# Fewer and larger transpose DMAs between windowed attention and a gated feed-forward layer

## The chip, the cores and the metric

The kernel runs on one core of a Trainium2 chip. The metric is device time in microseconds, the median of several executions of the same program. The engines are TensorE (PE, with its weight loads shown apart as PEld), VectorE (DVE), ScalarE (ACT), GpSimd (POOL) and SyncE (SP), which here only issues DMAs.

## What is computed

Windowed attention with four sink keys, and then a feed-forward layer with a gate. Sizes: batch 4, 8 heads, 768 positions, head size 64, window 128; 3072 tokens, model width 512, inner width 2048.

```python
scores = (q @ k.transpose(0, 1, 3, 2)) / sqrt(64)
rel = pos[:, None] - pos[None, :]
keep = (pos[None, :] < 4) | ((rel >= 0) & (rel < 128))
a = softmax(where(keep, scores, -1e9))
x = (a @ v).transpose(0, 2, 1, 3).reshape(3072, 512)
h = x @ w_in
out = (h * sigmoid(beta * h)) @ w_out
```

Inputs and output are float32. The products run in bfloat16 with float32 sums.

## The kernel before

The work is cut into 8 half batches of 384 tokens (`hb`, three blocks of 128), and each half batch into 4 units, a unit being two heads. Unit `u` is half batch `u // 4`, pair of heads `u % 4`.

For each half batch: q, k and v are loaded in float32 (`load`, line 543), three DMAs each, and cast to bfloat16 on whichever engine is free (`cast`, line 584). q and k must have the head dimension on partitions, so they are transposed into `qkT`. For half batches 0 to 2 (`CUT = 3`) TensorE does that (`T`, line 651). From the fourth on, SyncE issues crossbar transpose DMAs (`XP`, line 634): one for each of q and k and each block of 128 tokens, so six for a half batch, each with four 128x128 blocks, one block for each unit. Score products (`SC`, line 735) read `qkT` and write PSUM, ScalarE takes the exponential (line 747), GpSimd or VectorE masks (lines 755, 761, 765). The four sink keys have small products of their own (`first_keys`, line 623 on GpSimd, and `SS`, line 777). `AV` (lines 807 and 818) multiplies with v and divides into `onorm` (line 824), tokens on partitions. The feed-forward layer needs it transposed, as `xT`: by TensorE for the first three half batches (`OT`, line 844), then by one transpose DMA for each unit (line 838), of three blocks each. `HQ` is the first product of the feed-forward layer (line 862), with tanh on ScalarE (line 867) and the gate on VectorE (line 869); `OQ` is the second (line 882), whose result is copied and sent out (line 892, from GpSimd, and from SyncE for the last half batch).

The order of all this is not written out by hand. `_program` appends operations as its own clock says that they can run, choosing among transposes, scores, AV, H and O pieces (`head` and `background`); then `Graph.arrange` orders the operations of every engine once more with a list of costs: each has `ns`, and a DMA also `hold`, the time that it keeps its issuing engine. A DMA's landing is put at `dma_free + 1000`, with `dma_free = max(dma_free, at + 1100) + 1.15 * ns`. A q or k transpose has ns 950 and hold 1310, an xT transpose 750 and 1310. `Graph.resolve` turns the dependencies into semaphore waits, and every engine runs its own list in order. An instruction that waits holds back all that stand behind it on that engine.

Gates around the changed DMAs: `qkT` has room for three half batches (NT = 12 units), and `XP` of half batch hb is planned only when its chunk is cast and the units of hb - 2 are all scored; `x16` has two buffers, `onorm` five (NON), `xT` five half batches (NXT).

Of the kernel before, what the change touches and what calls it, by code (L numbers as in the profile page):

```python
# [4 lines left out]
BF16 = mybir.dt.bfloat16  # L5
F32 = mybir.dt.float32
# [356 lines left out]
def _program(nc, G, sb, ps, q, k, v, w_in, w_out, beta, out):  # L363
    NU = 2 * NPAIR
    NSTG, NX, NV, NT, NE, NON, NG, NTT, NOS, NWS = 2, 2, 3, 12, 7, 5, 3, 3, 4, 6
    NXT = 5
# [6 lines left out]
    maskT = sb("maskT", (128, 2, 128), BF16)  # L373
    beta_st = sb("beta_st", (16, 128), F32)
    ident32 = sb("ident32", (16, 16), F32)
    hbeta = sb("hbeta", (128, NM), F32)
    warm = sb("warm", (1, 1), F32)
    headm = sb("headm", (128, 2), BF16)
    xT = sb("xT", (128, 4, NXT * HALF), BF16)
    w_in16 = sb("w_in16", (128, 4, DF), BF16)  # L380
# [6 lines left out]
    vaug = sb("vaug", (128, NK, H, D + 1), BF16, NV)  # L387
    qkT = sb("qkT", (128, NT, 2, HALF), BF16)
    E = sb("E", (128, 4, 2, 128), BF16, NE)
# [5 lines left out]
    own = sb("own", (128, H), F32)  # L395
    onorm = sb("onorm", (128, NK, 2, D), BF16, NON)
    rden = sb("rden", (128, 2 * NK), F32, NON)
# [5 lines left out]
    tt = sb("t", (128, HALF), F32, NTT)  # L403
    osb = sb("osb", (128, NOUT), F32, NOS)
    P = ps("P", (128, 8, 512))

    def add(eng, fn, ns, r=(), w=(), x=(), dma=None, after=(), hold=550, chain=None):
# [111 lines left out]
    def beta_in():  # L519
        G.begin()  # L520
        b_ = take(1)
        add("pe", lambda e: nc.tensor.transpose(P[:, b_[0], 0:NM], beta_st[:, :], ident32[:, :]), 30,
            r=["beta_st", "ident32"], x=[("B", b_[0])])
        add("dve", lambda e: e.tensor_scalar(hbeta[:, :], P[:, b_[0], 0:NM], 0.5, None, ALU.mult), 80,
            w=["hbeta"], x=[("B", b_[0])])
        give(b_)
# [75 lines left out]
    def first_values_pe():  # L602
# [9 lines left out]
        give(bk)  # L612

    def qk_keys(u, name="qkT", every=NT):
        return [(name, u % every, a, c) for a in range(2) for c in range(NK)]

    def first_keys(hb, units):

        ks = hb // 2 % 2
        j0, n = units[0], len(units)  # L620
        z0 = (4 * hb + j0) % NT
        kd = kS[ks][:, 32 * j0:32 * (j0 + n)].rearrange("p (j a w) -> p j a w", a=2, w=16)[:, :, :, 0:NSINK]
        add("gp", lambda e: e.tensor_tensor(
            kd, qkT[:, z0:z0 + n, 1:2, 0:NSINK].to_broadcast([128, n, 2, NSINK]),
            headm[:, :].unsqueeze(1).unsqueeze(3).to_broadcast([128, n, 2, NSINK]), ALU.mult), 200,
            r=[("kS", ks), "headm0", "headm"] + [("qkT", z0 + j, 1, 0) for j in range(n)],
            w=[("kSd", ks, j) for j in units])

    def XP(hb, n, c):

        z0, i = 4 * hb % NT, "qk".index(n)
        src = x16[n][hb % NX][:, c, :, :].rearrange("p h d -> p (h d)")
        dst = qkT[:, z0:z0 + 4, i, c * 128:(c + 1) * 128]
        add("sp", lambda e: e.dma_start_transpose(dst, src), 950,
            r=[(n + "16", hb % NX, j, c) for j in range(4)], w=[("qkT", z0 + j, i, c) for j in range(4)],
            dma=f"x{n}{hb % 3}{c}", hold=1310)
        for j in range(4):
            mark(("qkTu", 4 * hb + j, i, c), ("qkT", z0 + j, i, c))
        if hb % 2 == 0 and (n, c) == ("k", 0):
            first_keys(hb, range(4))  # L640

    def T(u):
# [12 lines left out]
        if len(bs) == 2:  # L655
            for i in range(2):
                mp = P[:, bs[i], :].bitcast(BF16)[:, i * HALF:(i + 1) * HALF]
                any_of(copies(qkT[:, u % NT, i, :].rearrange("p (s j) -> p s j", j=NK),
                              mp.rearrange("p (j s) -> p s j", j=NK), {"dve": 470, "act": 380}),
                       w=[("qkT", u % NT, i, c) for c in range(NK)], x=[("B", bs[i])])  # L660
        else:
            mp = P[:, bs[0], :].bitcast(BF16)
            any_of(copies(qkT[:, u % NT, :, :].rearrange("p a (s j) -> p a s j", j=NK),
                          mp[:, 0:2 * HALF].rearrange("p (a j s) -> p a s j", a=2, j=NK), {"dve": 868, "act": 690}),
                   w=qk_keys(u), x=[("B", bs[0])])
# [48 lines left out]
    def SC(n):  # L714
# [4 lines left out]
        for j, t_ in enumerate(tiles):  # L719
# [3 lines left out]
            for (u, kb), cols in jobs.items():  # L723
                half = u // 4 % 2
                cols.sort()
                own_ = u if kb >= NK * half else u - 4
                kt = qkT[:, own_ % NT, 1, :]
                kc = (kb % NK) * 128
                q0, i0, nq = (cols[0][0] - NK * half) * 128, cols[0][1], len(cols)
                st = cols[1][1] - i0 if nq > 1 else 1  # L730
                for hh in range(2):
                    rows = slice(64 * hh, 64 * hh + 64)
                    bank = P[:, bs[2 * j + hh], :].rearrange("p (s w) -> p s w", w=128)
                    dst = bank[:, i0:i0 + st * (nq - 1) + 1:st, :]
                    add("pe", lambda e, dst=dst, kt=kt, kc=kc, rows=rows, q0=q0, nq=nq, u=u: e.matmul(  # L735
                        dst, kt[rows, kc:kc + 128],
                        qkT[rows, u % NT, 0, q0:q0 + 128 * nq].rearrange("p (s w) -> p s w", w=128),
                        start=True, stop=True), mm_ns(128 * nq) / 2 + 12,
                        r=qk_keys(u) + (qk_keys(own_) if own_ != u else []), x=[("B", bs[2 * j + hh])])
# [31 lines left out]
    def SS(hb, bank):  # L771
# [3 lines left out]
        for j in range(4):  # L775
            u = 4 * hb + j
            add("pe", lambda e, j=j, u=u: e.matmul(  # L777
                P[32 * j:32 * j + 32, bank, q0:HALF], kS[ks][:, 32 * j:32 * j + 32], qkT[:, u % NT, 0, q0:HALF],
                start=True, stop=True), 100 if j == 0 else (mm_ns(HALF - q0) if j == 3 else 5),
                r=[("kSd", ks, j)] + qk_keys(u), x=[("B", bank)])  # L780
# [16 lines left out]
    def AV(u):  # L797
# [5 lines left out]
        for m, ps in enumerate(parts(u)):  # L803
# [20 lines left out]
        add("dve", lambda e: e.tensor_tensor(  # L824
            onorm[on][:, :, :, :].rearrange("p m h d -> p (m h) d"), av[:, :, 0:D],
            rden[on][:, :].unsqueeze(2).to_broadcast([128, 2 * NK, D]), ALU.mult), dve_ns(HALF),
# [3 lines left out]
    def OT(u):  # L830
        G.begin()
        b, half, hp = where(u)
        on = u % NON
        t0 = (2 * b + half) % NXT * HALF
        if u >= 4 * CUT:
            dst = xT[:, hp, t0:t0 + HALF].rearrange("p (m t) -> p m t", m=NK)
            src = onorm[on][:, :, :, :].rearrange("p m h d -> p (m h d)")
            add("sp", lambda e: e.dma_start_transpose(dst, src), 750, r=[("on", on)],
                w=[("xT", hp, (2 * b + half) % NXT)], dma=f"xo{on}", hold=1310)
            return  # L840
        bs = take(1)
        mp = P[:, bs[0], :].bitcast(BF16)
        for m in range(NK):
            add("pe", lambda e, m=m: nc.tensor.transpose(  # L844
                mp[:, m * 128:(m + 1) * 128], onorm[on][:, m, :, :].rearrange("p h d -> p (h d)"), ident[:, :]),
                mm_ns(128), r=[("on", on), "ident"], x=[("B", bs[0])])
        any_of(copies(xT[:, hp, t0:t0 + HALF], mp[:, 0:HALF], {"dve": 407, "act": 370}),
               w=[("xT", hp, (2 * b + half) % NXT)], x=[("B", bs[0])])
        give(bs)
# [4 lines left out]
    def HQ(T_, m):  # L854
# [3 lines left out]
        bs = take(1)  # L858
        t0 = T_ % NXT * HALF
        hp = P[:, bs[0], 0:HALF]  # L860
        for c in range(4):
            add("pe", lambda e, c=c: e.matmul(  # L862
                hp, w_in16[:, c, m * 128:(m + 1) * 128], xT[:, c, t0:t0 + HALF],
                start=(c == 0), stop=(c == 3)), mm_ns(HALF),
# [47 lines left out]
    OS += [(T_, t, j) for T_ in range(1, NSB) for t in range(3) for j in range(4)]  # L912
    XPS = [(hb, n, c) for hb in range(CUT, NSB) for n in "qk" for c in range(NK)]
    n_cast, n_w, n_x = [0], [0], [0]
    BACKLOG, AHEAD, MARGIN = 6000, 300, 200

    def head(s):
# [26 lines left out]
        elif s == "AV":  # L944
            if i >= NU or i >= done["OT"] + NON or i >= units_scored() or n_cast[0] < 11 + 9 * (i // 4):
                return None
            t, tb = G.at(av_keys(i)), banks_at(1)
            fn = lambda: (AV(i), mark(("onu", i), ("on", i % NON)))
        elif s == "OT":
# [5 lines left out]
            if i // 4 >= NXT and done["H"] < NM * (i // 4 - NXT + 1):  # L955
                return None
            fn = lambda: (OT(i), mark(("xTu", i % 4, i // 4), ("xT", i % 4, i // 4 % NXT)))
        elif s == "H":
# [22 lines left out]
    def background():  # L981
# [3 lines left out]
        while moved:  # L985
# [29 lines left out]

            if n_x[0] < len(XPS):
                hb, n, c = XPS[n_x[0]]
                if n_cast[0] > CASTS.index(XPS[n_x[0]]) and units_scored() >= 4 * (hb - NT // 4 + 2):
                    XP(hb, n, c)
                    n_x[0] += 1  # L1020
                    moved = True
                    if n_x[0] % 6 == 0:
                        done["T"] += 4
# [43 lines left out]
    def beta_load():  # L1067
        add("sp", lambda e: e.dma_start(beta_st[:, :], beta.rearrange("(m p) -> m p", p=128)), 20, w=["beta_st"],
            dma="dbeta", chain=2)
# [93 lines left out]
```

## Time and profile before

| | us |
|---|---|
| median of 7 runs | 227.83 |
| lowest, highest | 226.26, 229.52 |
| profiled execution, in all | 227.83 |
| profiled execution, span | 226.1 |

| group, line | times | busy us | mean ns |
|---|---|---|---|
| first feed-forward product, L862 | 512 | 97.1 | 326 |
| second, L882 | 384 | 96.2 | 379 |
| attention times v, L818 | 352 | 17.8 | 193 |
| scores, L735 | 288 | 14.4 (on top of weight loads 9.4) | 230 |
| gate on VectorE, L869 | 128 | 70.3 | 552 |
| tanh on ScalarE, L867 | 128 | 74.1 | 583 |
| transposes of q and k by DMA, L634 | 30 | | 1269 a median issue |
| transposes of onorm by DMA, L838 | 20 | | 1256 a median issue |

The span is the time from the first to the last instruction of the program in the profiled execution; the device time is 1.7 us longer. TensorE's durations overlap, since a product starts before the end of the one ahead, so the starts tell more than the durations. The chain that ended last is TensorE work for 81% of the span; L882 is 37% of it and L862 33%.

### The profile page before, as it was taken

To read this page: it belongs to the slowest core of one execution; us is meant where nothing else is said; L and a number is where in the kernel's file an instruction comes from. 1 tells how busy PE (TensorE), PEld (TensorE's weight loads), DVE (VectorE), ACT (ScalarE), POOL (GpSimd) and SP (SyncE) were. 2 spreads that over 40 slices of the span, in tenths; PEclk is the share of its full clock that TensorE was granted. 3 is DMA by queue.
4 is the path that set the end of the run, shared out by engine and by line. 5 is a ranking of instruction groups with operands and counts; after the bars stand their busy time and mean duration, and the time that the engine had idled before them with its cause. 6 is when DMAs were issued, how large, how long until landed. Compare 5 with 4: busy or idle time off the path is not lost.

```text
span 226.1 us, 4583 instructions
## 1 busy us (share of the span) xinstructions
PE 215.7 (95%) x1802; PEld 124.0 (55%) x1802; DVE 138.2 (61%) x289; ACT 148.4 (66%) x241; POOL 78.2 (35%) x137
## 2 busy tenths in 40 slices
PE   8796986999999999999999999999999999999994
PEld 6574644656556565646555655545654665555541
DVE  1667879966668575669676644748864564633310
ACT  2595996657984687495577875587666936744431
POOL 6156649024470465048004451037002840000000
PEclk9999999999999999999999999999999999999999
DMA  5999999999989967589949986799448033011112
GB/s 144 240 290 355 323 306 394 392 265 226 159 187 261 193 122 197 128 186 219 197 84 200 213 177 146 148 226 246 106 93 180 0 85 80 0 46 49 46 48 93
DMA packets 96077, 39.86 MB, mean 176 GB/s; under 512 B 82024, under 2 KB 92280, under 8 KB 96056
## 3 DMA queue, kind: packets, MB, share of 16 engines
q1 hardware_dynamic: 94376, 34.07, 65.7%
q0 software_dynamic: 1680, 5.51, 7.5%
q8 instruction: 14, 0.23, 0.4%
q14 instruction: 7, 0.06, 0.1%
HBM read 27.37 MB, written 6.29 MB: 149 GB/s over the span
## 4 chain that ended last, share of the span: by engine, by line
PE 81%; SPq 10%; DMA 3%; DVE 3%; issue 0%; ACT 0%
PE P L882 37%; PE P L862 33%; SPq L543 6%; PE P L735 4%; SPq L554 4%; PE P L818 4%; DMA v_stage<-in_v_dram 3%; DVE E L765 2%; PE P L807 1%; PE P L777 1%; PE P L651 1%; PE P L844 1%; DVE vaug L478 0%; ACT osb L473 0%; DVE onorm L824 0%
## 5 line engine op out<-in xcount | busy, mean ns | idle before, releaser
L867 ACT ACTIVATE t<-P,hbeta 128x384 f32<-128x384 f32 x128 | 74.1, 583 | 48.9 <-PE P L862 44.9
L869 DVE SCALAR_TENSOR_TENSOR g<-t,P 128x384 bf16<-128x384 f32 x128 | 70.3, 552 | 51.6 <-ACT t L867 47.6
L862 PE MATMUL P<-xT,w_in 128*128 128x384 bf16 x512 | 97.1, 326 | 0.7 <-DVE g L869 0.5
L882 PE MATMUL P<-w_out,g 128*128 128x512 bf16 x384 | 96.2, 379 | 0.0
L862 PEld LDWEIGHTS P<-xT,w_in 128*128 128x128 bf16 x512 | 48.4, 98 | 38.9 <-DVE g L869 1.3
L761 POOL TENSOR_SCALAR_AFFINE_SELECT E<-E 128x512 bf16<-128x512 bf16 x60 | 40.2, 691 | 60.0 <-ACT E L747 59.7
L882 PEld LDWEIGHTS P<-w_out,g 128*128 128x128 bf16 x384 | 36.0, 98 | 35.1 <-DVE g L869 0.8
L747 ACT ACTIVATE E<-P 128x1024 bf16<-128x1024 f32 x44 | 43.2, 1026 | 4.1 <-PE P L735 3.7
L892 POOL DMA_DIRECT2D out_dram<-osb x21 | 11.8, 562 | 43.5 <-ACT osb L473 43.3
L818 PE MATMUL P<-vaug,E 128*128 128x65 bf16 x352 | 17.8, 193 | 2.1 <-DVE E L765 1.5
L824 DVE TENSOR_TENSOR onorm<-P,rden 128x384 bf16<-128x384 f32 x32 | 17.8, 558 | 1.1
L473 ACT ACTIVATE osb<-P 128x512 f32<-128x512 f32 x17 | 10.1, 597 | 12.7 <-PE P L882 12.6
L818 PEld LDWEIGHTS P<-vaug,E 128*128 128x128 bf16 x352 | 15.7, 97 | 4.6 <-DVE E L765 2.4
L735 PE MATMUL P<-qkT 64*128 64x128 bf16 (+1 forms) x288 | 14.4, 230 | 0.8 <-DVE qkT L478 0.8
L735 PEld LDWEIGHTS P<-qkT 64*128 64x128 bf16 x288 | 9.4, 94 | 9.5 <-issue 3.9
L807 PE MATMUL P<-vS,ES 128*128 128x130 bf16 x64 | 12.9, 220 | 0.0
L755 DVE TENSOR_TENSOR E<-E,maskS 128x512 bf16<-128x512 bf16 x16 | 7.7, 480 | 8.1 <-ACT E L747 8.1
L478 DVE CAST q<-q_stage 128x512 bf16<-128x512 f32 (+1 forms) x15 | 7.6, 518 | 6.8 <-DMA q_stage<-in_q_dram 6.8
L1073 PE MATMUL P<-ones 128*128 128x256 bf16 x60 | 9.9, 321 | 1.1 <-POOL ones L484 1.1
L478 DVE CAST vaug<-v_stage 128x512 bf16<-128x512 f32 x16 | 7.6, 491 | 1.6 <-DMA v_stage<-in_v_dram 1.6
L473 ACT ACTIVATE qkT<-P 128x384 bf16<-128x384 bf16 (+1 forms) x12 | 6.3, 574 | 3.4 <-PE P L651 3.4
L822 DVE RECIPROCAL rden<-P 128x6 f32<-128x6 f32 x32 | 6.1, 189 | 4.0 <-PE P L818 3.9
(58 smaller groups left out, 117.2 us busy)
## 6 DMA issues: line engine op xcount, KB each, us to landing
v_stage<-in_v_dram SPq DMA_DIRECT2D x24, 256.0 KB, 4.5
out_dram<-osb POOLq DMA_DIRECT2D x21, 256.0 KB, 3.1
q_stage<-in_q_dram SPq DMA_DIRECT2D x15, 256.0 KB, 5.1
k_stage<-in_k_dram SPq DMA_DIRECT2D x15, 256.0 KB, 5.0
wst<-in_moe_w_in_dram SPq DMA_DIRECT2D x5, 512.0 KB, 6.1
wst<-in_moe_w_out_dram SPq DMA_DIRECT2D x4, 512.0 KB, 6.9
g<-in_moe_w_out_dram SPq DMA_DIRECT2D x4, 512.0 KB, 7.1
q_stage<-in_q_dram SPq DMA_DIRECT2D x2, 768.0 KB, 8.7
```

The lines of the kernel that those rows point to most:

```text
L473: return lambda e: e.activation(dst, src, AF.Copy, bias=0.0, scale=scale)
L478: return lambda e: e.tensor_copy(dst, src)
L735: add("pe", lambda e, dst=dst, kt=kt, kc=kc, rows=rows, q0=q0, nq=nq, u=u: e.matmul(dst, kt[rows, kc:kc + 128], qkT[rows, u % NT, 0, q0:q0 ...
L747: add("act", lambda e, src=src, dst_=dst_: e.activation(dst_, src, AF.Exp, bias=0.0, scale=SCALE), act_ns(1024), w=[("E", z)] + [("m", z, ...
L761: alts = {"gp": (lambda e, dd=dd, sg=sg: e.affine_select(dd, dd, [[0, 4], [sg, 128]], ALU.is_ge, 0.0, base=min(sg, 0), channel_multiplier= ...
L807: add("pe", lambda e, m=m, c0=c0: e.matmul(A[:, c0:c0 + 2 * (D + 1)], ES[u // 4 % 2][:, m * 128:(m + 1) * 128], vS[b % 2][:, 2 * hp:2 * hp ...
L818: e.matmul(A[:, c0:c0 + D + 1], E[t_ % NE][:, i, hh, :], vaug[vz][:, kb % NK, 2 * hp + hh, :], start=a, stop=o, skip_group_check=True), 31,
L824: add("dve", lambda e: e.tensor_tensor(onorm[on][:, :, :, :].rearrange("p m h d -> p (m h) d"), av[:, :, 0:D], rden[on][:, :].unsqueeze(2) ...
L862: add("pe", lambda e, c=c: e.matmul(hp, w_in16[:, c, m * 128:(m + 1) * 128], xT[:, c, t0:t0 + HALF], start=(c == 0), stop=(c == 3)), mm_ns ...
L867: add("act", lambda e: e.activation(tt[ti][:, :], hp, AF.Tanh, bias=0.0, scale=hbeta[:, m:m + 1]), act_ns(HALF) + 93, r=["hbeta"], w=[("t" ...
L869: add("dve", lambda e: e.scalar_tensor_tensor(gt[T_ % NG][:, m, :], tt[ti][:, :], 1.0, hp, ALU.add, ALU.mult), dve_ns(HALF), r=[("t", ti)] ...
L882: add("pe", lambda e, m=m: e.matmul(P[:, bk, :], gt[T_ % NG][:, m, t * 128:(t + 1) * 128], w_out16[:, m, :], start=(m == 0), stop=(m == NM ...
```

## The change

The six q and k transposes of a half batch become two: one takes all three blocks of q for all four units, one all of k. The `xT` transposes are made for two units at a time. That makes 10 DMAs in place of 30, and 10 in place of 20, with the same bytes.

Three layouts follow. A half batch's slot of `qkT` is flat: for the half batches that TensorE transposes it is ordered unit, q or k, token, as it was; for the others q or k, block, unit, token, so that a unit's three blocks lie 512 elements apart. `xT` is ordered half batch, pair of heads, token. `onorm` comes in pairs of units, with six in place of five. To make room for the sixth, the small staging tile of beta shares the last output buffer `osb`. A slot that still has the old order is given up as a whole: the q transposes of half batches 3 to 5 also wait for the old readers of k.

The planner is given other costs: ns 1300 and hold 1500 for a q or k transpose, 900 and 1300 for a pair of units. `XP` is planned when all three chunks of q, or of k, are cast. `AV` may run ahead by six units, counted from the last full pair that is transposed.

```diff
-    NSTG, NX, NV, NT, NE, NON, NG, NTT, NOS, NWS = 2, 2, 3, 12, 7, 5, 3, 3, 4, 6
+    NSTG, NX, NV, NT, NE, NON, NG, NTT, NOS, NWS = 2, 2, 3, 12, 7, 6, 3, 3, 4, 6
...
-    qkT = sb("qkT", (128, NT, 2, HALF), BF16)
+    qkT = sb("qkT", (128, NT // 4, 8 * HALF), BF16)
...
-    onorm = sb("onorm", (128, NK, 2, D), BF16, NON)
+    onorm2 = sb("onorm", (128, 2, NK, 2, D), BF16, NON // 2)
+    onorm = [onorm2[i // 2][:, i % 2, :, :, :] for i in range(NON)]
...
+    beta_st = osb[NOS - 1][0:16, 0:128]
...
+    XNS, XHOLD, ONS, OHOLD = (1300, 1500, 900, 1300)
...
+    def slot(hb):
+        x = qkT[:, hb % (NT // 4), :]
+        if hb < CUT:
+            return x.rearrange("p (z a c t) -> p a c z t", z=4, a=2, t=128)
+        return x.rearrange("p (a c z t) -> p a c z t", a=2, c=NK, t=128)
+
+    def qk_of(u, i):
+        return slot(u // 4)[:, i, :, u % 4, :]
...
-    def XP(hb, n, c):
+    def XP(hb, n):
 
         z0, i = 4 * hb % NT, "qk".index(n)
-        src = x16[n][hb % NX][:, c, :, :].rearrange("p h d -> p (h d)")
-        dst = qkT[:, z0:z0 + 4, i, c * 128:(c + 1) * 128]
-        add("sp", lambda e: e.dma_start_transpose(dst, src), 950,
-            r=[(n + "16", hb % NX, j, c) for j in range(4)], w=[("qkT", z0 + j, i, c) for j in range(4)],
-            dma=f"x{n}{hb % 3}{c}", hold=1310)
+        src = x16[n][hb % NX][:, :, :, :].rearrange("p c h d -> p (c h d)")
+        dst = qkT[:, hb % (NT // 4), i * 4 * HALF:(i + 1) * 4 * HALF].rearrange("p (b t) -> p b t", t=128)
+        old = [("qkT", z0 + j, 1, c) for j in range(4) for c in range(NK)] if i == 0 and hb < CUT + NT // 4 else ()
+        add("sp", lambda e: e.dma_start_transpose(dst, src), XNS,
+            r=[(n + "16", hb % NX, j, c) for j in range(4) for c in range(NK)],
+            w=[("qkT", z0 + j, i, c) for j in range(4) for c in range(NK)], dma=f"x{n}{hb % 3}", hold=XHOLD, after=old)
...
-                        dst, kt[rows, kc:kc + 128],
-                        qkT[rows, u % NT, 0, q0:q0 + 128 * nq].rearrange("p (s w) -> p s w", w=128),
+                        dst, kt[rows, kc, :], qk_of(u, 0)[rows, q0:q0 + nq, :],
...
         if u >= 4 * CUT:
-            dst = xT[:, hp, t0:t0 + HALF].rearrange("p (m t) -> p m t", m=NK)
-            src = onorm[on][:, :, :, :].rearrange("p m h d -> p (m h d)")
-            add("sp", lambda e: e.dma_start_transpose(dst, src), 750, r=[("on", on)],
-                w=[("xT", hp, (2 * b + half) % NXT)], dma=f"xo{on}", hold=1310)
+            if u % 2:
+                dst = xT[:, x_, hp - 1:hp + 1, :].rearrange("p h (m t) -> p (h m) t", t=128)
+                src = onorm2[on // 2][:, :, :, :, :].rearrange("p u m h d -> p (u m h d)")
+                add("sp", lambda e: e.dma_start_transpose(dst, src), ONS, r=[("on", on - 1), ("on", on)],
+                    w=[("xT", hp - 1, x_), ("xT", hp, x_)], dma=f"xo{on // 2}", hold=OHOLD)
             return
...
-            if i >= NU or i >= done["OT"] + NON or i >= units_scored() or n_cast[0] < 11 + 9 * (i // 4):
+            if i >= NU or i >= (done["OT"] if done["OT"] < 4 * CUT else done["OT"] // 2 * 2) + NON or i >= units_scored() or n_cast[0] < 11 + 9 * (i // 4):
...
-                if n_cast[0] > CASTS.index(XPS[n_x[0]]) and units_scored() >= 4 * (hb - NT // 4 + 2):
-                    XP(hb, n, c)
+                if n_cast[0] > CASTS.index((hb, n, NK - 1)) and units_scored() >= 4 * (hb - NT // 4 + 2):
+                    XP(hb, n)
```

## What was expected of it

> **What bounds the kernel now.** I read the page's engine rows first, then its slices, then the table of windows, then the waits of TensorE from 57 us on, then SyncE's issues. The engine rows say that TensorE's matmul row is busy 95% of the span, but a matmul's modelled end lies beyond the next one's start, so busy alone does not prove a full engine. The windows and the waits do.
>
> ```profile
> span 226.1 us, 4583 instructions
> PE 215.7 (95%) x1802; PEld 124.0 (55%) x1802; DVE 138.2 (61%) x289; ACT 148.4 (66%) x241; POOL 78.2 (35%) x137
> PE   8796986999999999999999999999999999999994
> PEclk9999999999999999999999999999999999999999
> DMA  5999999999989967589949986799448033011112
> ```
>
> ```profile
> 0.00:57.00 57.00, 49.92 (x478) 31.87 (x479) 40.40 (x86) 39.60 (x67) 27.51 (x56) 1.00 1.01 293
> 57.00:218.00 161.00, 161.00 (x1305) 90.15 (x1304) 97.83 (x205) 107.57 (x173) 50.70 (x81) 1.00 0.67 139
> 218.00:226.10 8.10, 4.82 (x23) 1.97 (x21) 0.00 (x0) 1.19 (x2) 0.00 (x0) 1.00 0.25 97
> ```
>
> The columns after the length are busy time of PE, weight load, DVE, ACT and POOL, then the granted clock, the DMA share and GB/s. From 57 to 218 us, where every transpose DMA lies (first 57.5, last 187.2), TensorE has no idle time at all and the clock is 1.00; the answer on TensorE's own waits in that window is an empty list. The starts of the long products agree: four w_out products take 0.86 us from first start to the next group (the groups of the chain), 216 ns each for 512 columns; four w_in products take 0.65, 162 ns for 384 columns, one column in 0.42 ns in both. So the middle is work and not waiting. The TensorE idle time is 7.1 us before 57 us and 3.3 us after the last matmul.
>
> **The DMAs that change.**
>
> ```profile
> L634 SPq DMA_TRANSPOSE qkT<-q x15: 1188/1269/2164, 57.5 to 165.2; - x15
> L634 SPq DMA_TRANSPOSE qkT<-k x15: 1254/1269/2577, 60.7 to 166.5; - x15
> L838 SPq DMA_TRANSPOSE xT<-onorm x20: 1181/1256/1950, 86.8 to 187.2; - x20
> ...
> SPq L838 <- DVE g L869: 23.4, 10, 10.2
> SPq L838 <- DVE onorm L824: 8.5, 3, 3.4
> ```
>
> The three numbers are the shortest, median and longest time in ns that one issue holds SyncE's queue. A qkT transpose moves four 128x128 blocks, an xT one three: 1269 against 1256 ns, so a block more costs 13 ns of issue. The data go fast: in the 0.3 us windows in which only one xT transpose runs (181.0 and 183.0 us) DMA share is 1.06 at 217 to 218 GB/s. A block is 32.8 KB, so 0.15 us a block.
>
> **Part 1: 30 q and k transposes become 10.** Removed: 30 x 1.27 = 38 us of SyncE. Added: 10 issues of twelve blocks, not in this trace. From below an issue costs the fixed 1.27 us; from above it grows with blocks, 3 x 1.27 = 3.8. By the nearest rows it is 1.27 + 8 x 0.013 = 1.37, which I take. [...]
>
> Landing: a four-block transpose lands 2.5 us after its issue when nothing is ahead of it, which is 1.27 of issue, 0.6 of data and 0.6 of the rest. Twelve land at 1.37 + 1.8 + 0.6 = 3.8 us, and with proportional issue at 3.8 + 1.8 + 0.6 = 6.2.
>
> What matters is the last block. Now six issues, which start 1.30 apart at best (four xT ones from 112.75 to 117.95), need 6 x 1.30 + 1.2 = 9.0 us from first issue to last landing; two need 1.37 + 3.8 = 5.2, and 0.4 more because two streams of 1.8 us follow one another. The merged q must wait for its third cast, which is up to 4.8 us later than the first (151.4 and 156.2 us in the last half batch), but the last landing now waits for that cast too. Set that against when it is used. From the last landing to the first score product (line 735) of that half batch there are 7.2, 8.8, 5.7, 8.7 and 4.0 us for half batches 3 to 7; the last is 166.50 + 2.5 = 169.0 to 172.98. So the time removed was covered by 4 us or more of other matmuls, and is worth 0 on the path; if the cover were gone the two holds booked and the measured ones would differ by 2 x (1.37 - 1.5), which is under 0.3.
>
> **Part 2: 20 xT transposes become 10.** SyncE gives up 20 x 1.26 = 25 us and gets 10 x (1.26 + 3 x 0.013) = 13. The bounds for one are 1.26 and 2.5. The first unit of each pair now waits for the second: 0.7 us in the burst at 105.7, 106.4, 107.1, 107.8, at most 2.8 (127.7 to 130.5). The w_in products need all four units, so only the second counts, and it lands 2.4 + 3 x 0.16 = 2.9 us after its issue, 0.5 later than now. Cover: last landing to the first w_in product of that half batch (counted, 64 products each) is 5.4, 2.4, 3.2, 4.1 and 3.3 us. The smallest is 119.1 to 121.5, and there the four transposes stood behind six qkT issues until 112.75 although their data were ready at 108.4; that queue is now shorter by 6 x 1.30 - 2 x 1.37 = 5.1 us. Worth 0 too; if the cover were gone, 0.5 us at each of five places.
>
> **Part 3: waits.** Behind the pair's wait on SyncE stand the v loads and the next half batch's q and k loads. It waits 31.9 us there already (the two rows above), and 38 + 25 - 14 - 13 = 36 us come free in the same queue, so the loads go earlier rather than later. On POOL the sink keys (line 623, twice, 238 ns) wait for all of k in place of its first third: some 4 us later, with mask operations and output DMAs behind it. POOL is 35% busy, and the product that reads the keys comes at 99.9 and 154.0 us, at least 12 us after k has landed. The added wait on old k readers falls on products that ended before 83 us, at least 20 us before the q that needs it: 0. A sixth onorm buffer makes the reuse distance in pairs no shorter than before: 0.
>
> **Part 4: reads with another step.** The 180 score products and 20 sink products of half batches 3 to 7 read qkT in runs of 128 columns, 256 bytes, which are apart by 1 KB now. No row has such a read. A gain is excluded: the columns are as many. From above, if each jump cost 50 ns (no jump is shown; a 128-column pair of products takes 54), 40 products with one jump and 12 with two would cost 3.2 us. The products already write in steps at full pitch, so I take 0.
>
> **Part 5: another order.** Lines of the planner are fed other costs (1300/1500 and 900/1300), so from the first changed issue on (57 us) the order of all engines may differ; before it I expect no change. TensorE's products are the same in number. What order can move is the entry into the half-array score products: the next start after a w_out product is 310 ns off in place of 216 (the idle rows of weight load before line 735, 0.3 to 0.4 us, are its sign). At about 0.19 us for entry and exit, three bursts more or fewer are 0.6 us.
>
> Sum: 0 + 0 + 0 + 0, give or take 0.6. The profiled execution has span 226.1 and 227.83 us in all, which is also the median of the seven runs (226.26 to 229.52). So 227.8. [...]
>
> **Rivals.** *A new wait for the merged transposes (slower).* The planner books 2 x 1.5 us of SyncE where it booked 6 x 1.31, and may bring the scores forward by 4.9 us. If the issue really grows with the blocks (3.8), nothing of that is real, and the streaming adds 1.2: 6.1 late against covers of 4.0 to 8.8, so 2.1 us at half batch 7 and 0.4 at 5; the pairs behind (2.5 held, 1.3 booked) are each 1.2 late, twice, against 2.4 to 5.4, which adds about 1 where the replanned order is tight: 3.5 us, 231.3. It decides from an issue of about 2.9 us. For it: no twelve-block issue is in the trace, and held issues reach 2.6. Against: 13 ns a block. Chance 0.22, with part 4's upper end in it.
>
> *The freed queue helps (faster).* There are 0 us of TensorE waits to take in the window that changes; fewer bursts give 0.6, and the remaining idle lies before 57 us or behind the last product. Over 1% is 2.3 us, which I can find nowhere; chance 0.05, at 225.3.
>
> *The change hardly happens.* The planner may keep the same order of products behind the same gates (scores done, buffers free), with half the DMAs: 227.8, inside the main case. Main case in all 0.73, own range 226.6 to 229.2.
>
> **The numbers.** About 1% is what a measurement of this kernel can tell from no change. Faster by more than that: 0.05 from the faster case and 0.01 of the main one. Slower: 0.22 and 0.01 of the main one, less 0.01 of the slow rival that ends under 1%. Same: 0.72. The range leaves out the faster case and the worse half of the slow one: 226.0 to 231.2.
>
> **What would show it.** Right: no waits in TensorE's list from 57 to 218 us; ten q and k issues of about 1.4 us, landing in about 4; ten pair issues of 1.3 landing in about 3. Wrong: issues near 3 us or more, or a TensorE or weight load wait on a transpose of q, k or onorm; a pitch above 54 ns a pair in the score products of late half batches; idle slices of PE after slice 10; or a busy PE before 57 us that differs from 49.9.

## The result, and the profile after

The changed kernel takes 229.51 us (median of 24 runs, 228.17 to 232.18) against 227.66 before (61 runs); the ratio is 1.0086, with a 95% interval of 1.0067 to 1.0106. It is slower by 1.85 us. The forecast was no change, at 227.8. Some executions take 2 to 3 us longer, most of them at a lower granted clock (four of the kernel before took 230.22 to 230.93 us at 0.982 to 0.985, beside a median of 227.70); the ratios leave them out, and so are not quite the quotients of the medians.

The page of the changed kernel, profiled at 228.57 us in all. Line numbers moved: 634 is 646 now, 838 is 855, 735 is 751, 862 is 878 and 882 is 898.

```profile
span 226.8 us, 4544 instructions
PE 215.7 (95%) x1802; PEld 123.5 (54%) x1802; DVE 139.8 (62%) x290; ACT 147.3 (65%) x240; POOL 77.5 (34%) x137
PE   8887886999999999999999999999999999999994
PEclk9999999999999999999999999999999999999999
DMA  5999999999999999999999999531130211011112
```

TensorE does the same 215.7 us of work. The DMA row is full up to slice 25 and then nearly empty, where before it had holes in the middle and work up to slice 31: the loads do go earlier. The table of windows of the same kernel:

```profile
0.00:57.00 57.00, 49.32 (x477) 31.44 (x478) 41.62 (x85) 39.26 (x67) 27.54 (x56) 1.00 1.04 290
57.00:218.00 161.00, 160.76 (x1302) 89.75 (x1301) 98.17 (x206) 106.56 (x172) 49.97 (x81) 1.00 0.69 140
218.00:226.80 8.80, 5.67 (x27) 2.35 (x24) 0.00 (x0) 1.45 (x3) 0.00 (x0) 0.97 0.23 89
```

In the stretch that the change was meant for, TensorE idles for 161.00 - 160.76 = 0.24 us, of which the view of its waits from 57 us on shows one of 0.2:

```profile
PE P L898 <- DVE g L885: 0.2, 1, 0.2
```

That can't be 1.85. The first 57 us have 0.6 us less TensorE work in them than before (49.92), though there no engine's list of instructions differs from before but in the name of beta's tile: the first row that differs stands at about 57 us. The changed DMAs (issue in ns: shortest, median and longest):

```profile
L646 SPq DMA_TRANSPOSE qkT<-q x5: 1497/1579/2879, 61.4 to 136.5; - x5
L646 SPq DMA_TRANSPOSE qkT<-k x5: 1575/2808/3892, 63.1 to 132.5; - x5
DMA to landing us min/median/max: 3.8/5.2/6.2
...
L855 SPq DMA_TRANSPOSE xT<-onorm x10: 1209/1392/2053, 92.2 to 174.6; - x10
DMA to landing us min/median/max: 2.7/3.9/6.5
```

### The profile page after: what moved, and what is told of

Read it like the earlier page. It is cut to its first block, busy times and chain, and to the rows that moved or that the text cites. A ratio compares the mean times of both kernels' runs of the same rounds, so it can differ in the third digit from the quotient of the medians.

```text
span 226.8 us, 4544 instructions
## 1 busy us (share of the span) xinstructions
PE 215.7 (95%) x1802; PEld 123.5 (54%) x1802; DVE 139.8 (62%) x290; ACT 147.3 (65%) x240; POOL 77.5 (34%) x137
## 4 chain that ended last, share of the span: by engine, by line
PE 76%; SPq 7%; DMA 7%; DVE 5%; ACT 3%; issue 1%; POOL 0%
PE P L898 35%; PE P L878 31%; DMA k_stage<-in_k_dram 7%; SPq L545 5%; PE P L751 4%; PE P L834 3%; ACT E L762 2%; DVE E L780 2%; SPq L556 2%; PE P L823 1%; DVE g L885 1%; DVE onorm L840 1%; PE P L667 1%; DVE qkT L480 1%; PE P L792 1%
## 5 line engine op out<-in xcount | busy, mean ns | idle before, releaser
L885 DVE SCALAR_TENSOR_TENSOR g<-t,P 128x384 bf16<-128x384 f32 x128 | 69.3, 551 | 50.0 <-ACT t L883 47.8
L878 PE MATMUL P<-xT,w_in 128*128 128x384 bf16 x512 | 98.3, 327 | 1.4 <-DVE g L885 1.2
L475 ACT ACTIVATE osb<-P 128x512 f32<-128x512 f32 x19 | 11.3, 597 | 14.1 <-PE P L898 14.1
L480 DVE CAST q<-q_stage 128x512 bf16<-128x512 f32 (+1 forms) x16 | 7.1, 457 | 8.7 <-DMA q_stage<-in_q_dram 8.7
L480 DVE CAST vaug<-v_stage 128x512 bf16<-128x512 f32 x17 | 9.7, 573 | 1.5 <-DMA v_stage<-in_v_dram 1.4
L770 DVE TENSOR_TENSOR E<-E,maskS 128x512 bf16<-128x512 bf16 x16 | 8.5, 539 | 2.9 <-ACT E L762 2.9
L477 POOL TENSOR_SCALAR_AFFINE_SELECT q<-q_stage 128x512 bf16<-128x512 f32 x5 | 3.5, 706 | 17.5 <-DMA q_stage<-in_q_dram 17.5
L780 DVE TENSOR_TENSOR E<-E,maskT 128x512 bf16<-128x512 bf16 x12 | 8.2, 716 | 0.9 <-ACT E L762 0.9
```

Source lines behind the costliest of these rows:

```text
L480: return lambda e: e.tensor_copy(dst, src)
L780: alts["dve"] = (lambda e, dd=dd, tri=tri: e.tensor_tensor(dd, dd, tri, ALU.mult), 335)
L878: add("pe", lambda e, c=c: e.matmul(hp, w_in16[:, c, m * 128:(m + 1) * 128], xT[:, T_ % NXT, c, :], start=(c == 0), stop=(c == 3)), mm_ns( ...
L885: add("dve", lambda e: e.scalar_tensor_tensor(gt[T_ % NG][:, m, :], tt[ti][:, :], 1.0, hp, ALU.add, ALU.mult), dve_ns(HALF), r=[("t", ti)] ...
```

## The experiments

Three theories led the first four runs. A: the planner books the merged transposes too low, so loads are pulled ahead and the casts and masks behind them are late. B: the large streams cost time themselves. C: the coarser release does, since a whole q or k, or a pair of units, must be ready.

**The old bookings on the merged DMAs.**

```diff
-    XNS, XHOLD, ONS, OHOLD = (1300, 1500, 900, 1300)
+    XNS, XHOLD, ONS, OHOLD = (2850, 3930, 1500, 2620)
```

> The changed kernel, but its merged transposes are booked with the planner at what the single ones were booked at in sum: ns 3 x 950 = 2850 and hold 3930 for q or k, 1500 and 2620 for a pair. Theory A (bookings too low: the planner thinks the DMA queue free 4.9 us earlier per half batch, pulls the loads ahead, and puts casts and masks behind loads that land late, so that the gate on VectorE is late): the time returns to that of before, ratio 0.998 to 1.003, the DMA share of 76 to 97 us falls from 1.21 to about 0.75, and the waits of the three casting engines for loads fall from some 28 us in 76 to 148 us to under 5. Rival B (streams of twelve blocks themselves hold up other transfers and land late): the ratio stays at 1.007 to 1.010, whatever is booked. Rival C (waiting for a whole q or a pair, the coarser release): stays at 1.006 or more, with waits that trace to onorm, qkT or xT.

Measured: 228.92 us, ratio 1.0077 (1.0056 to 1.0099). The row of 76 to 97 us, in the changed kernel and then here:

```profile
76.00:97.00 21.00, 20.76 (x190) 12.02 (x188) 15.32 (x36) 16.87 (x27) 10.95 (x19) 1.00 1.21 217
76.00:97.00 21.00, 20.68 (x189) 12.30 (x193) 15.35 (x32) 16.45 (x26) 10.45 (x18) 1.00 0.87 187
```

The DMA share (last but one) fell from 1.21 to 0.87, the time did not come back. Theory A does not carry the loss.

**Low bookings on the single DMAs of before.**

```diff
-        add("sp", lambda e: e.dma_start_transpose(dst, src), 950,
+        add("sp", lambda e: e.dma_start_transpose(dst, src), 433,
...
-            add("sp", lambda e: e.dma_start_transpose(dst, src), 750, r=[("on", on)],
+            add("sp", lambda e: e.dma_start_transpose(dst, src), 450, r=[("on", on)],
```

> The kernel before with its 50 single transposes, but booked in the DMA queue at the merged kernel's sum: ns 433 in place of 950 for q and k, 450 in place of 750 for xT; holds left at 1310. Theory A: slower by 0.4 to 0.9% although no DMA is merged, with a DMA share above 1.0 in 76 to 120 us and waits for loads on the casting engines. Rivals B and C: no change, ratio 0.998 to 1.002.

Measured: 234.98 us, ratio 1.0346 (1.0292 to 1.0399), far more than theory A said. Its waits of TensorE from 57 us on, which the kernel before has none of (the three longest):

```profile
PE P L735 <- DMA qkT<-k: 1.8, 1, 1.8
PE P L807 <- DVE g L869: 1.3, 1, 1.3
PE P L735 <- DVE g L869: 1.3, 1, 1.3
```

The columns are the sum, the number and the longest. A score product waits for a transpose of k, so here a booking that is too low shows in TensorE's list. The changed kernel's list has 0.2 us from 57 us on, and so its bookings are not too low in that sense.

**One half of the change at a time.** First only q and k merged (the xT transposes made one by one again), then only the pairs of xT (six single q and k transposes again).

```diff
-            if u % 2:
-                dst = xT[:, x_, hp - 1:hp + 1, :].rearrange("p h (m t) -> p (h m) t", t=128)
+            dst = xT[:, x_, hp, :].rearrange("p (m t) -> p m t", t=128)
...
```

> Only q and k are merged (2850 booked as 1300, hold 1500); the xT transposes are single as before (750, 1310). Theory A: 3.55 of the 4.9 us less booked per half batch are here (1.15 x (6 x 950 - 2 x 1300)), so about 0.7 of the loss, ratio 1.005 to 1.007. Rival C by pairs: ratio under 1.002, since the pairs are gone. Rival B: 1.006 or more, the large streams being all here.

> Only the xT transposes are made in pairs (900, 1300); q and k have six single DMAs for a half batch as before (950, 1310). Theory A: 1.07 of the 4.9 us less booked (1.15 x (4 x 750 - 2 x 900) is 1.38), so a loss of about a quarter, ratio 1.001 to 1.004. Rival C by pairs: 1.006 or more. Rival B: about 1.001.

Measured: 1.0064 (1.0035 to 1.0093) with q and k alone, 1.0092 (1.0064 to 1.0120) with the pairs alone. Theory A had expected 1.001 to 1.004 of the pairs and theory B 1.001; theory C had expected under 1.002 of q and k alone. Each half by itself costs what the whole does, within the intervals. So the cost was looked for in what the four slow merged kernels (changed, old bookings, and the two halves) share. That is neither DMA, but the storage: each has six onorm buffers and beta in `osb`. Per partition the change takes away 512 bytes (`beta_st`) and adds 768 (onorm) and 32 (a rden of 24 bytes in its slot): `g`, the weight staging `wst`, `t` and `osb`, which are allocated after them, move by 288 = 256 + 32 bytes. By the order of allocation all four began on a multiple of 256 bytes before. No view shows addresses, so what the runs can test is the move; "on the grid" below means the place, up to whole steps of 256 bytes, that these tiles have in the kernel before.

That gave theory L: weight loads that are written 32 bytes off this grid are slower, and they set the pace before 57 us.

**The grid given back to the changed kernel, taken from the kernel before, and given back under the old bookings.**

```diff
-    rden = sb("rden", (128, 2 * NK), F32, NON)
+    rden = sb("rden", (128, 2 * NK), F32, NON - 1)
...
     osb = sb("osb", (128, NOUT), F32, NOS)
+    rden.append(sb("rdenZ", (128, 2 * NK), F32))
```

```diff
     rden = sb("rden", (128, 2 * NK), F32, NON)
+    pad = sb("pad", (128, 8), F32)
```

> The changed kernel with one thing moved: the sixth rden buffer (24 bytes) is allocated last, so that g, the weight staging, t and the output buffers, which the change shifted by 288 bytes a partition, begin on a multiple of 256 bytes again, as before. Every engine's list is the same as in the changed kernel. Theory L (the shift off the 256-byte grid makes the 8.4 MB of weight loads slower, and these set the pace up to 57 us): about 1 us comes back, ratio to before 1.002 to 1.005, last weight landing at 45.4 in place of 45.9 to 47.3 us. Rival A/C (the loss is all in the order after 57 us): no change, ratio 1.007 to 1.010.

> The kernel before with an unused tile of 32 bytes a partition ahead of g, so that g, the weight staging, t and the output buffers begin 32 bytes off the 256-byte grid, as in the changed kernel. Lists unchanged. Theory L: slower by about 1 us, ratio 1.003 to 1.006, with the last weight landing 0.5 to 2 us later than 45.3. Rival A/C: ratio 0.998 to 1.002.

> The first experiment (merged DMAs booked at the old sums) with the sixth rden moved as well, so aligned. Theory L with a rest that comes from the order: ratio 1.000 to 1.004, since the part from 58.3 us on was 164.9 us there against 164.3 before. Rival A/C: as the first experiment, 1.006 to 1.010.

Measured: 1.0024 (0.9986 to 1.0061) for the changed kernel on the grid, 1.0027 (0.9993 to 1.0061) for the kernel before off it, 1.0031 (1.0007 to 1.0056) for the old bookings on it, against 1.0077. All go the way of theory L, and so do the last landings of a weight in the profiles (44.8 us in the first, 45.85 in the second, against 45.3 before, though this measure does not hold up: 46.6 in a later run with the weights on the grid), but the first two intervals reach to 1, and the second ratio is just under what was expected. The first and third lie below 1.0086 and 1.0077 by 0.6 and 0.5%.

**The staging of q, k and v on the grid as well, and another offset.** The q, k and v staging is 64 bytes off the grid in before and after alike. In the kernel before, rden and `own` were moved ahead of `xT`; in the changed one rden was, with `own` put last. That is 192 bytes in either, so that everything that a load writes is on the grid (other tiles move with it, and `qkT`, which the transposes write, goes off). A third run takes a pad of 64 in place of 32 bytes ahead of `g`.

```diff
+    rden = sb("rden", (128, 2 * NK), F32, NON)
+    own = sb("own", (128, H), F32)
     xT = sb("xT", (128, 4, NXT * HALF), BF16)
...
```

> The kernel before with rden and own (192 bytes in all) allocated ahead of xT in place of after onorm: the float32 staging of q, k and v, 64 bytes off the 256-byte grid in before and in the changed kernel alike, now begins on it, and g, the weight staging and the output buffers stay on it. Lists unchanged. Theory L with a grid of 256 bytes: the loads of q, k and v, most of them rows of 256 bytes, go faster, the first 57 us shrink, ratio 0.985 to 0.997. Theory L with a grid of 64 bytes (32 off costs, 64 off does not): ratio 0.998 to 1.002, and the rate of 5 to 46 us stays near 330 GB/s.

> The changed kernel with rden allocated ahead of xT and own last, so that staging of q, k, v, the weights, g and the output buffers all begin on a multiple of 256 bytes. Lists unchanged. Theory L with a grid of 256 bytes: below the aligned variant of the first alignment run (1.0024), 0.988 to 0.999. With a grid of 64 bytes: 1.001 to 1.005, as there.

> The kernel before with an unused tile of 64 bytes a partition ahead of g: g, the weight staging, t and the output buffers 64 bytes off the 256-byte grid. Lists unchanged. Grid of 256 bytes: as with the shift of 32, 1.003 to 1.006 and 308 to 320 GB/s in 5 to 46 us. Grid of 64 bytes: 0.998 to 1.002 and 325 to 337 GB/s.

Measured: 227.07 us and 0.9968 (0.9939 to 0.9998) for the kernel before, 226.93 us and 0.9952 (0.9924 to 0.9980) for the changed one, 1.0040 (1.0018 to 1.0062) for the pad of 64. So 64 bytes off cost as 32 do within the intervals, and a grid of 64 bytes is excluded. No run has an offset of 128, so the runs by themselves do not tell a grid of 256 bytes from one of 128. The mean time of the 78,720 packets of 256 bytes, which are most of these loads and all transposes (counted in the traces), falls from 21.1 ns before to 18.5 in the first of these profiles and 19.0 in the second. The two kernels differ by less than their intervals, and both are slightly faster than the kernel before.

**Which of the moved tiles it is.** Two pads put only `g` and `wst`, or only `t` and `osb`, 32 bytes off; the edit of the first:

```diff
     rden = sb("rden", (128, 2 * NK), F32, NON)
+    pad = sb("pad", (128, 8), F32)
...
+    pad2 = sb("pad2", (128, 56), F32)
     tt = sb("t", (128, HALF), F32, NTT)
```

> The kernel before with 32 unused bytes a partition ahead of g and 224 ahead of t: only g and the weight staging, into which the weight loads are written, lie 32 bytes off the 256-byte grid; t and the output buffers are on it. Lists unchanged. If the weight loads carry the cost: ratio 1.003 to 1.006, as with all of them shifted, and 308 to 320 GB/s in 5 to 46 us. If the output stores or the reads of t carry it: 0.998 to 1.002.

> The kernel before with 32 unused bytes a partition ahead of t: only t and the output buffers lie 32 bytes off the 256-byte grid; g and the weight staging are on it. Lists unchanged. If the weight loads carry the cost: 0.998 to 1.002 and 325 to 337 GB/s in 5 to 46 us. If the output stores or t carry it: 1.003 to 1.006.

Measured: 1.0047 (1.0022 to 1.0072) with only g and the weight staging off, 0.9978 (0.9948 to 1.0007) with only t and the output buffers off. A lower clock is no rival here: among the executions whose granted clock reads 0.996 or more, the mean is 1.1 us above that of the kernel before beside it with all four tiles 32 bytes off, 1.0 with 64, 1.2 with only g and the weight staging off, and 0.3 below it with only t and osb off.

The expected rates of 5 to 46 us do not tell the runs apart: 310 GB/s with the weights off, but also 320 with t and osb off, 321 with all on the grid and 321 with the pad of 64. A shorter stretch does. SyncE issues three weight loads into the spare third of `g`, with q and k of half batch 1 between them, and then v; no issue waits for another engine there. The view of tile `v_stage` from 20 to 23.5 us shows how long a v issue is held behind the weight loads, and how long it then takes to land. The kernel before:

```profile
L543 SPq DMA_DIRECT2D v_stage<-in_v_dram x2: 1145/1726/2307, 21.3 to 22.5; - x2
DMA to landing us min/median/max: 7.1/7.2/7.2
```

The changed kernel:

```profile
L545 SPq DMA_DIRECT2D v_stage<-in_v_dram x2: 1306/1869/2432, 21.1 to 22.5; - x2
DMA to landing us min/median/max: 7.4/7.6/7.7
```

The changed kernel with the sixth rden moved:

```profile
L546 SPq DMA_DIRECT2D v_stage<-in_v_dram x3: 1146/2294/2323, 19.6 to 23.1; - x3
DMA to landing us min/median/max: 6.1/6.9/7.0
```

The kernel before with only g and the weight staging off the grid:

```profile
L545 SPq DMA_DIRECT2D v_stage<-in_v_dram x2: 1314/1870/2426, 21.9 to 23.3; - x2
DMA to landing us min/median/max: 7.4/7.6/7.7
```

And with only t and the output buffers off:

```profile
L544 SPq DMA_DIRECT2D v_stage<-in_v_dram x2: 1146/1714/2281, 21.5 to 22.7; - x2
DMA to landing us min/median/max: 6.8/6.9/6.9
```

The shortest issue in each is the first v load right behind the weights: 1145, 1146 and 1146 ns where the weights lie on the grid, and 1306 and 1314 where they do not. In the other nine profiles the same issue takes 1146 to 1183 on it (four) and 1307 to 1318 off it (five). From the landing of half batch 1's q to that of its first v there are always the same five transfers, 2.5 MB. In the fourteen profiles this takes 7.09 to 7.45 us in the seven with g on the grid, and 7.84 to 8.15 us in the seven with g off it, with no overlap: some 0.7 us more.

The packets say it directly. Their mean times in that stretch, counted in the traces (no view lists them):

| packets | g on the grid, seven profiles | g off it, seven |
|---|---|---|
| weights, 1024 bytes | 46.0 to 46.8 ns | 51.5 to 51.7 ns |
| k, 768 bytes | 36.0 to 39.2 | 41.2 to 41.4 |
| v, 256 bytes | 18.0 to 19.9 | 21.9 to 22.5 |

So the loads beside the weights get slower with them, though their own place is the same; the 36.0 and 18.0 are those of the two runs with their staging on the grid too. What reads the weights does not get slower: the two casts of weights on ScalarE take 1.06 to 1.08 and 1.05 to 1.06 us in all fourteen profiles.

## Why the prediction was wrong

The step that failed is the last sentence of part 3, "A sixth onorm buffer makes the reuse distance in pairs no shorter than before: 0", with part 5's "before it I expect no change" (the order there did stay, the time did not). The buffer was priced as a wait alone. Its bytes, with those of beta's tile, moved the destination of every weight load by 32 bytes off the grid, in the stretch where the DMA share is 1.01 and TensorE idles 7.1 us (both before, up to 57 us). The code gives all sizes, so this could have been counted before. The cost: 1.0086 against 1.0024 on the grid is 0.62%, 1.4 us of the 1.85, give or take 0.4% by the two intervals; the kernel before with only g and the weight staging off pays 0.47% (0.22 to 0.72), 1.1 us.

The traces show the cost in the packets of the weight loads in the stretch above, 51.5 to 51.7 in place of 46.0 to 46.8 ns for 1024 bytes; why 32 or 64 bytes off the grid cost that, no run shows. The prediction did not weigh it.

The other steps:

- Part 1, issue: 1.37 us for twelve blocks. The shortest is 1.50, and three more take 1.58. Against the shortest and the median of four blocks (1.19 and 1.27), a block adds 39 ns and not 13. The five longest q and k issues, 2.6 to 3.9, began with three or four of SyncE's transfers still under way, the other five with one to three. Landing: 3.8 forecast, 3.8 the shortest, but 5.2 the median. The cover held: no score product waits for a transpose.
- Part 2: 1.30 and 2.9 us forecast, 1.39 in the median (shortest 1.21) and 2.7 to 6.5 measured, worth 0 as said.
- Part 3, SyncE: the last v load is issued at 139.7 us; before, the last three went out from 167.8 us on, so the loads did go earlier. That gains nothing, as TensorE was full (161.00 of 161.00 us busy from 57 to 218 us before).
- Part 4, reads with another step: 0 was right. The score products keep a mean of 230 ns.
- Part 5, order: 26 bursts of scores in place of 25. From the first score product of half batch 2 to the start of the last w_out product there are 164.33 us before, and within 0.01 in the five other profiles with the same lists. The changed lists take 165.09, and 164.68 in both variants on the grid. So the order itself costs 0.35 us, within the 0.6 allowed; the one burst more, at 0.19, is about half of that, and the rest was not placed. The other 0.4 us are waits of TensorE for the gate in this one profile: a cast of k on ScalarE stands 1.2 us before a load, the exponentials and masks behind it. That is what is left of theory A. With 1.1 us for the weights these come to about 1.85, but the first of them is known to half a us only.

The slow rival, merged transposes that land behind their plan, is not what happened: with the weights on the grid, both halves of the change are in and the time is that of before within the interval. That the number was only 0.8% off says nothing for the sum: what cost the time had no term in it. What stays open: the weight stream off the grid shows 0.7 us in the stretch that can be compared; the rest of the 1.1 to 1.4 was not traced to single loads. Nor does one profile of each kernel show it as a whole: the first score product of half batch 2 starts at 56.8 to 59.3 us in the seven with g on the grid and at 57.8 to 59.8 in the other seven (58.12 before, 58.20 changed), so the size rests on the medians of the runs.

## What to carry to other kernels

An edit that adds, drops or resizes a buffer moves every tile allocated after it; count the bytes and ask where the destinations of the large loads come to lie, above all where the loads set the pace. Here a move of `g` and `wst` by 256 bytes left the weight packets at 46.0 to 46.8 ns (the changed kernel with the sixth rden moved), and moves by 32, 64 and 288 put them at 51.5 to 51.7; no other distance was tried. When two halves of a change each cost as much as the whole, look for what both have besides their purpose. The fastest version here is the changed kernel with all load destinations on the grid, 226.93 us, though the kernel before takes 227.07 with them there.

## What was not expected of the hardware

A transpose DMA of twelve blocks holds the issuing queue at least 1.50 us, one of four 1.19, one of three 1.18: three times the data for 0.31 us. Offsets of 32 and of 64 bytes a partition slow the weight packets alike, to 51.6 and 51.7 ns in that stretch, from 46.7 before. And with the same lists on every engine, the 164.33 us of the dense part come back within 0.01 us in six profiles, while the time of the whole varies by 2% from run to run: in these profiles all of the difference lies in the part before. The two that reach it last, at 58.9 and 59.8 us, have a granted clock of 0.97 up to 57 us, the other four 1.00.
